# A transformer block on one core: x in four loads, LN1's norms on the vector engine, fp32 dummy matmuls, an earlier gate, and one earlier LN2 chunk

## The chip, the cores and the metric

The kernel runs on one core of a Trainium2 chip. Times are device microseconds (us) of one execution. The granted clock is the share of PE's full clock that the chip let it have, read from the profile: 1.0 is full. "Faster" or "slower" needs 2%; effects here are read as ratios to the kernel before, run on the same chip in the same rounds.

Engines: PE is the tensor engine (PEld its weight loads), DVE the vector engine, ACT the scalar engine, POOL the GpSimd engine, SP the engine that issues most transfers. "Modulating" is the multiplication by 1 + scale after a layer norm (in LN2 the shift is added too). A "fall" is a stretch in which the granted clock drops to a half. The "chain" is the work that ended last, followed back in the profile from the last instruction to what released each step.

## The reference

A DiT block with x of 2 x 256 x 1152 in bf16 (512 tokens, in four tiles of 128), two heads and a hidden size of 4608:

```python
mod = (_silu(c) @ w_mod).reshape(B, 6, 1, D)
shift_a, scale_a, gate_a, shift_m, scale_m, gate_m = [mod[:, i] for i in range(6)]
h = _layernorm(x) * (1 + scale_a) + shift_a            # LN1
q, k, v = split(h @ wqkv)
a = softmax(q k^T * Dh**-0.5) v @ wo
x = x + gate_a * a
h2 = _layernorm(x) * (1 + scale_m) + shift_m           # LN2
return x + gate_m * (_gelu(h2 @ w_fc1) @ w_fc2)
```

(The attention and split lines are shortened.)

## The kernel before

In the traces of this case DVE and ACT take up their instructions in program order (under e11, ACT starts tile 1's root 1.24 us later, behind its passes over tile 2; in the changed kernel DVE does four norms, 1.43 us, before the modulate that PE waits for). All weights stream through five buffers of 2.65 MB. Dummy matmuls, whose results nobody reads, are there to keep PE busy until its first inputs land (in the profile they run from 1.20 to 6.69 us, and the first scale weights land at 9.05). The parts that matter here (short statements joined on one line and comments added, cuts marked):

```python
for t in range(TPB):                                   # tiles 0, 1
    nc.sync.dma_start(x_sb[:, t, :], x_v[:, 0, t, :])
nc.sync.dma_start(x_sb[:, TPB:2 * TPB, :], x_v[:, 1, :, :])   # tiles 2 and 3 together
...
def warm(n, dst):                                      # dummy matmuls on zeros
    for _ in range(n):
        nc.tensor.matmul(dst[:], zeros[:, 0:P], zeros[:], start=True, stop=True)
warm(4, pwarm)
... # transpose of c, silu
def norm1(t, c0, c1, eng):                             # (x - mean) * rstd
    eng.tensor_scalar(xns[t][:, c0:c1], x_sb[:, t, c0:c1], mv1[:, t, 0:1], rstd1[:, t:t + 1],
                      op0=ALU.subtract, op1=ALU.mult)
...
CUT = 2 * P
warm(13, pwarm)
for j in range(NPD): stats_piece(0, j)                 # DVE bn_stats of tile 0
sqrt1(0); stats_piece(1, 0); recip1(0)
norm1(0, 0, CUT, nc.vector); norm1(0, CUT, D, nc.gpsimd)
act_stats(ACT.Identity, dsum)                          # tile 2's sums, on ACT
stats_piece(1, 1); stats_piece(1, 2); sqrt1(1)
act_stats(ACT.Square, dsq)
stats_piece(3, 0); recip1(1)
norm1(1, 0, CUT, nc.vector); norm1(1, CUT, D, nc.gpsimd)
stats_piece(3, 1)
add = scale_group(0)                                   # PE: 18 two-column matmuls
pt_a = transpose_x([0, 1], BT[0]); add()               # PE transposes of chunks 0, 1
modulate(pt_a, 0, 0, 0, 0, "d"); modulate(pt_a, 1, 1, 0, 0, "a")
... # statistics and first norms of tiles 3 and 2
k_step(0, 0, N); k_step(1, 0, N)                       # K projection, chunk by chunk
```

A K step multiplies one 128-column chunk of the modulated input with six weight blocks. Later, gate_a is computed in the V stage (after eight of twelve V groups), goes through DRAM to be broadcast to all partitions, and multiplies the output projection's result, from which LN2's statistics come:

```python
for i, (pnl, t) in enumerate(v_order):
    ...
    v_group(pnl, t)
    if i == 7:
        gate_a = gate_natural(0, w_gate_a)
...
BETWEEN = {2: ((0, "d"), (1, "d"), (2, "a"), (3, "a")), 3: ((8, "d"),)}   # LN2 modulates
...
nc.vector.tensor_tensor(tmp[:], pacc[:], gate_a[:, b, c0:c1], op=ALU.mult)
```

Of the kernel before, what the change touches and what calls it, by code (L numbers as in the profile page):

```python
# [8 lines left out]
FP32 = mybir.dt.float32  # L9
BF16 = mybir.dt.bfloat16  # L10
ACT = mybir.ActivationFunctionType
# [8 lines left out]
def kernel(  # L20
# [11 lines left out]
    nc = tc.nc  # L32
    B, N, D = x.shape
# [3 lines left out]
    P = 128  # L37
    T = B * N
    NT = T // P
    TPB = N // P  # L40
# [19 lines left out]
    def acc_tile(shape, name, dt=FP32):  # L60
        return psum.tile(shape, dt, name=name, tag="acc", bufs=6)

    def aux_tile(shape, name, dt=FP32):
        return psum.tile(shape, dt, name=name, tag="aux", bufs=2)


    x_v = x.rearrange("b (p l) d -> p b l d", l=TPB)
# [4 lines left out]
    wmod_v = w_mod.rearrange("(k p) n -> p k n", p=P)  # L72
# [3 lines left out]
    S_SHIFT_A, S_SCALE_A, S_GATE_A, S_SHIFT_M, S_SCALE_M, S_GATE_M = range(6)  # L76

    def wide_tile(name):
        return wide.tile([P, KD, D], BF16, name=name, tag="wide")


    x_sb = act.tile([P, NT, D], BF16, name="x_sb", tag="x_sb")
    c_sb = act.tile([B * KD, P], BF16, name="c_sb")
    nc.scalar.dma_start(c_sb[:], c_v)
    for t in range(TPB):
        nc.sync.dma_start(x_sb[:, t, :], x_v[:, 0, t, :])
    nc.sync.dma_start(x_sb[:, TPB:2 * TPB, :], x_v[:, 1, :, :])

    zeros = const.tile([P, T], BF16, name="zeros")
    nc.vector.memset(zeros[:], 0.0)  # L90
# [9 lines left out]
    KM1 = 6  # L100
# [17 lines left out]
    def load_rows(name, view, col0):  # L118
        w = wide_tile(name)
        for r in range(0, KD, 3):  # L120
            load = nc.sync.dma_start(w[:, r:r + 3, :], view[:, r:r + 3, col0:col0 + D])
            first_load.setdefault(name, load.ins)
        return w
# [5 lines left out]
    for (j0, j1), rows in zip(SHG, QROWS):  # L129
        nc.sync.dma_start(  # L130
            w_shift_a[:, :, j0 * P:j1 * P],
            wmod_v[:, :, S_SHIFT_A * D + j0 * P:S_SHIFT_A * D + j1 * P],
        )
        for r0, r1 in rows:
            nc.sync.dma_start(w_q[:, r0:r1, :], wqkv_v[:, r0:r1, 0:D])
    w_v = load_rows("w_v", wqkv_v, 2 * D)
    w_gate_a = load_rows("w_gate_a", wmod_v, S_GATE_A * D)
    w_o = load_rows("w_o", wo_v, 0)
    w_f1 = [None] * 4

# [15 lines left out]
    pwarm = acc_tile([P, T], "pwarm")  # L156


    def warm(n, dst):
        for _ in range(n):  # L160
            nc.tensor.matmul(dst[:], zeros[:, 0:P], zeros[:], start=True, stop=True)

    warm(4, pwarm)
    nc.tensor.transpose(pc[:], c_sb[:], ident[0:B * KD, 0:B * KD])
    nc.scalar.activation(
        sT[:, :, 0:B].rearrange("p k b -> p b k"), pc[:].rearrange("p (b k) -> p b k", b=B), ACT.Silu,
# [9 lines left out]
    def stats_piece(t, j):  # L176
        nc.vector.bn_stats(stats1[t][:, j, :], x_sb[:, t, j * PW:(j + 1) * PW])
        if j == NPD - 1:
            nc.vector.bn_aggr(mv1[:, t, :], stats1[t][:].rearrange("p a b -> p (a b)"))
# [4 lines left out]
    dsq = small.tile([P, 1], FP32, name="dsq", tag="dsq", bufs=1)  # L184
# [3 lines left out]
    def act_stats(f, dst):  # L188
        nc.scalar.activation(
            xns[T_ACT][:], x_sb[:, T_ACT, :], f, bias=pivot, scale=-1.0, accum_out=dst[:],  # L190
        )

    def act_stats_finish():
        nc.vector.scalar_tensor_tensor(
            dm2[:], dsum[:], -1.0 / (D * D), dsum[:], op0=ALU.mult, op1=ALU.mult
        )
        nc.vector.scalar_tensor_tensor(
            mv1[:, T_ACT, 1:2], dsq[:], 1.0 / D, dm2[:], op0=ALU.mult, op1=ALU.add
        )
        nc.vector.scalar_tensor_tensor(  # L200
            mv1[:, T_ACT, 0:1], dsum[:], -1.0 / D, pivot, op0=ALU.mult, op1=ALU.add
        )

    def sqrt1(t):
        nc.scalar.activation(rstd1[:, t:t + 1], mv1[:, t, 1:2], ACT.Sqrt, bias=eps_t[:], scale=1.0)

    def recip1(t):
        nc.vector.reciprocal(rstd1[:, t:t + 1], rstd1[:, t:t + 1])

    def norm1(t, c0, c1, eng):  # L210
        eng.tensor_scalar(
            xns[t][:, c0:c1], x_sb[:, t, c0:c1], mv1[:, t, 0:1], rstd1[:, t:t + 1],
            op0=ALU.subtract, op1=ALU.mult,
        )
# [22 lines left out]
    def modulate(pt, i, k, b, j0, eng):  # L237
        dst, src, sc = hT0[:, k, b * N:(b + 1) * N], pt[:, i, j0:j0 + N], scale_a[:, k, b:b + 1]
        if eng == "d":
            nc.vector.tensor_scalar_mul(dst, src, sc)  # L240
        else:
            nc.scalar.mul(dst, src, sc)
# [38 lines left out]
                start=(k == 0), stop=(k == KD - 1),  # L281
            )

    CUT = 2 * P
    BT = [range(b * TPB, (b + 1) * TPB) for b in range(B)]

    def both(pt, k):
# [6 lines left out]
    sqrt1(0)  # L294
    stats_piece(1, 0)
    recip1(0)
    norm1(0, 0, CUT, nc.vector)
    norm1(0, CUT, D, nc.gpsimd)
    act_stats(ACT.Identity, dsum)
    stats_piece(1, 1)  # L300
    stats_piece(1, 2)
    sqrt1(1)
    act_stats(ACT.Square, dsq)
    stats_piece(3, 0)
    recip1(1)
    norm1(1, 0, CUT, nc.vector)
    norm1(1, CUT, D, nc.gpsimd)
    stats_piece(3, 1)
    add = scale_group(0)
    pt_a = transpose_x([0, 1], BT[0])  # L310
    add()
    modulate(pt_a, 0, 0, 0, 0, "d")
    modulate(pt_a, 1, 1, 0, 0, "a")
    stats_piece(3, 2)
    sqrt1(3)
    act_stats_finish()
    sqrt1(2)
    recip1(3)
    norm1(3, 0, CUT, nc.vector)
    recip1(2)  # L320
    norm1(2, 0, CUT, nc.vector)
    k_step(0, 0, N)
    k_step(1, 0, N)
    pt_c = transpose_x([0, 1], BT[1])
# [5 lines left out]
    add()  # L330
    modulate(pt_b, 0, 2, 0, 0, "d")
    modulate(pt_b, 1, 3, 0, 0, "a")
    norm1(3, CUT, D, nc.vector)
    norm1(2, CUT, D, nc.vector)
    k_step(1, N, T)
    pt_d = transpose_x([2, 3], BT[1])
    modulate(pt_d, 0, 2, 1, 0, "d")
# [111 lines left out]
    def gate_natural(g, wg):  # L449
        pn = aux_tile([P, CTW], "pg")  # L450
        for k in range(KD):
            for i in range(4):
                nc.tensor.matmul(
                    pn[32 * i:32 * i + B, :], sT[:, k, 0:B], wg[:, k, i * CTW:(i + 1) * CTW],
                    start=(k == 0), stop=(k == KD - 1), tile_position=(0, 32 * i),
                )
        nat = work.tile([P, CTW], BF16, name="nat", tag="nat", bufs=1)
        for i in range(4):
            rows = slice(32 * i, 32 * i + B)
            if i % 2 == 0:  # L460
                nc.vector.tensor_copy(nat[rows, :], pn[rows, :])  # L461
            else:
                nc.scalar.copy(nat[rows, :], pn[rows, :])
            nc.gpsimd.dma_start(gates_dram[g, :, i * CTW:(i + 1) * CTW], nat[rows, :])  # L464
        return broadcast_gate(g)
# [4 lines left out]
    def q_mm(m, k):  # L470
        if k == 0:
            pq[m] = acc_tile([P, T], "pq")
        nc.tensor.matmul(  # L473
            pq[m][:], w_q[:, k, m * P:(m + 1) * P], hT[:, k, :],
            start=(k == 0), stop=(k == KD - 1), skip_group_check=True,
        )
        if k == KD - 1:
            evac(qT[:, m, :], pq[m][:], attn_scale)
# [7 lines left out]
    for m in range(KM1, KD):  # L486
        for k in range(KD):
            q_mm(m, k)

    def half(h):  # L490
        return slice(h * HP, (h + 1) * HP)
# [66 lines left out]
    for i, (pnl, t) in enumerate(v_order):  # L558
        if i < len(softmaxes):
            transposed = softmaxes[i]()  # L560
        v_group(pnl, t)
        if i == 7:
            gate_a = gate_natural(0, w_gate_a)

    w_shift_m = load_rows("w_shift_m", wmod_v, S_SHIFT_M * D)
    tc.add_manual_dep(first_load["w_shift_m"], transposed.ins.name, WAIT_FOR, reason="transposes first")
# [40 lines left out]
    def ln2_modulate(b, k, eng="d"):  # L607
        h = hT[:, k, b * N:(b + 1) * N]
        if eng == "a":
            return nc.scalar.activation(  # L610
                h, h, ACT.Identity, bias=shift_m[:, k, b:b + 1], scale=scale_m[:, k, b:b + 1],
            )
        return nc.vector.tensor_scalar(  # L613
            h, h, scale_m[:, k, b:b + 1], shift_m[:, k, b:b + 1], op0=ALU.mult, op1=ALU.add,
        )
# [34 lines left out]
        )  # L650


    BETWEEN = {2: ((0, "d"), (1, "d"), (2, "a"), (3, "a")), 3: ((8, "d"),)}

    def ln2_stats(t, i):
        nc.vector.bn_stats(stats2[t][:, i, :], x1[:, t, i * PW:(i + 1) * PW])  # L656
        if i == NPD - 1:
            nc.vector.bn_aggr(mv2[:, t, :], stats2[t][:].rearrange("p a b -> p (a b)"))
            ln2_normalize(t, t % 2 == 1, BETWEEN.get(t, ()))

    order = [(t, i) for t in range(NT) for i in range(NPD)]
    for o, (t, i) in enumerate(order):
        last = o == len(order) - 1
        if last:
            ln2_modulate(0, 4)
        wo_group(t, i, i < NPD - 1)
        if o == 2:
            vec_section(sT, w_shift_m, shift_m)
        if o == 5:
            vec_section(sT, w_scale_m, scale_m)  # L670
            nc.vector.tensor_scalar_add(scale_m[:, :, 0:B], scale_m[:, :, 0:B], 1.0)
        if o:
            ln2_stats(*order[o - 1])
        if last:
            ln2_modulate(0, 5, "a")
            ln2_modulate(0, 7, "a")
            ln2_modulate(0, 6)
    ln2_stats(*order[-1])
# [68 lines left out]
    for gi, (n, t, c0, cw) in enumerate(groups):  # L747
# [3 lines left out]
        for kk in range(KF):  # L751
# [4 lines left out]
                start=(kk == 0), stop=(kk == KF - 1),  # L756
# [11 lines left out]
    for ins in list(nc.cur_bb.bb.instructions)[first_traced:]:  # L768
        eng = ins.engine
# [38 lines left out]
```

## Time and profile before

249.81 us median of four runs (248.34 to 249.99). PE is busy for 237.6 of the 247.5 us span (96%). Of the rest, 3.6 us follow the last matmul; the waits that the profile names are listed here whole (engine, line, what it waited for: us in total, times, longest us):

```profile
PE pm L224 <- DMA w_scale_a<-in_w_mod_dram: 2.4, 1, 2.4
PE pwarm L161 <- DVE eps_t L94: 1.2, 1, 1.2
PE pacc L697 <- DVE hT L613: 0.6, 1, 0.6
PE pacc L697 <- ACT hT L610: 0.6, 1, 0.6
PE pk L250 <- DVE big L240: 0.5, 1, 0.5
PE pt L234 <- DVE xn L211: 0.5, 1, 0.5
```

The first line is PE waiting for the first scale weights after the dummies have run out. Lines 3 and 4 are waits of fc1 (L697) for LN2's modulates, lines 5 and 6 waits of the K stage.

The second loss doesn't show as idle time. In the view of windows of the kernel before, each line is one microsecond; after the length come the busy times of PE, PEld, DVE, ACT and POOL with their instructions, then the granted clock of PE, the share of the DMA engines and GB/s:

```profile
10.00:11.00 1.00, 0.58 (x6) 0.52 (x6) 0.95 (x3) 0.47 (x1) 1.00 (x1) 1.00 1.12 323
11.00:12.00 1.00, 1.00 (x8) 0.76 (x6) 0.84 (x7) 0.58 (x2) 1.00 (x1) 0.58 1.13 330
12.00:13.00 1.00, 0.54 (x4) 0.08 (x2) 0.83 (x3) 0.00 (x0) 0.79 (x1) 0.50 1.19 304
...
17.00:18.00 1.00, 0.99 (x8) 0.75 (x8) 0.29 (x2) 0.00 (x0) 0.00 (x0) 0.51 1.23 334
18.00:19.00 1.00, 1.00 (x11) 0.90 (x10) 0.13 (x1) 0.47 (x1) 0.00 (x0) 1.00 1.15 252
```

From within the second window on, PE works at half its clock, and is "busy" all the same. A K step of six 128x256 matmuls takes 1.44 us there.

Around LN2, from the timeline (up to 110 us; start, us, engine, line, operation, and in brackets the idle time before it and what ended it):

```profile
86.34 1.02 DVE L647 TENSOR_TENSOR tmp<-pacc,gate 128x384 f32<-128x384 f32 x2 [4.92 <-DMA gate<-gates_dram]
...
102.10 3.43 PE L697 MATMUL pacc<-hT,w_f 128*128 128x256 bf16 x30 [0.62 <-DVE hT L613]
...
106.10 4.09 PE L697 MATMUL pacc<-hT,w_f 128*128 128x256 bf16 x36 [0.57 <-ACT hT L610]
```

DVE can't start on the output projection's results until the gate arrives at 86.3 us, though the first result was there 3.7 us earlier (at 82.6); it is still behind when fc1 starts, and PE waits twice.

### The profile page before, as it was taken

To read this page: it belongs to the slowest core of one execution; us is meant where nothing else is said; L and a number is where in the kernel's file an instruction comes from. 1 tells how busy PE (TensorE), PEld (TensorE's weight loads), DVE (VectorE), ACT (ScalarE), POOL (GpSimd) and SP (SyncE) were. 2 spreads that over 40 slices of the span, in tenths; PEclk is the share of its full clock that TensorE was granted. 3 is DMA by queue.
4 is the path that set the end of the run, shared out by engine and by line. 5 is a ranking of instruction groups with operands and counts; after the bars stand their busy time and mean duration, and the time that the engine had idled before them with its cause. 6 is when DMAs were issued, how large, how long until landed. Compare 5 with 4: busy or idle time off the path is not lost.

```text
span 247.5 us, 3960 instructions
## 1 busy us (share of the span) xinstructions
PE 237.6 (96%) x1685; PEld 142.7 (58%) x1695; DVE 92.7 (37%) x199; ACT 61.1 (25%) x118; POOL 32.2 (13%) x39
## 2 busy tenths in 40 slices
PE   8599999999999999899999999999999999999994
PEld 2366444456657656678864444444566666666673
DVE  4842452316434189943000999970011000000001
ACT  5622431235134313455322333222000000000000
POOL 1900000000031043300000000001021222111111
PEclk9959999999999999999999999999999999999999
DMA  6999999992469999256999999199730000000000
GB/s 227 324 313 332 378 373 391 390 391 85 68 213 399 390 393 206 48 98 223 389 391 392 358 326 329 33 322 327 209 111 16 19 17 16 19 16 20 27 19 17
DMA packets 48637, 53.29 MB, mean 215 GB/s; under 512 B 9571, under 2 KB 36459, under 8 KB 48619
## 3 DMA queue, kind: packets, MB, share of 16 engines
q1 hardware_dynamic: 41168, 50.14, 60.3%
q10 hardware_dynamic: 6939, 1.71, 4.5%
q0 software_dynamic: 512, 1.19, 1.4%
q8 instruction: 13, 0.21, 0.4%
q14 instruction: 5, 0.04, 0.1%
HBM read 50.14 MB, written 1.19 MB: 207 GB/s over the span
## 4 chain that ended last, share of the span: by engine, by line
PE 79%; DMA 9%; DVE 5%; ACT 2%; issue 1%; POOL 1%; ACTq 1%; SPq 0%; DVEq 0%; POOLq 0%
PE pacc L753 28%; PE pacc L697 27%; PE pq L473 7%; PE pk L250 5%; PE pacc L550 5%; DMA w_scale_a<-in_w_mod_dram 3%; DMA gate<-gates_dram 3%; PE pk L279 2%; DMA gates_dram<-nat 2%; PE ps_s L508 2%; DMA hT<-xn 1%; DVE tmp L647 1%; PE pt L234 1%; DVE stats L656 1%; ACT xn L632 1%
## 5 line engine op out<-in xcount | busy, mean ns | idle before, releaser
L697 PE MATMUL pacc<-hT,w_f 128*128 128x256 bf16 (+1 forms) x427 | 70.4, 325 | 1.5 <-DVE hT L613 0.6
L753 PE MATMUL pacc<-w_f,gT 128*128 128x384 bf16 (+2 forms) x468 | 70.5, 314 | 0.0
L753 PEld LDWEIGHTS <-gT 128*128 128x128 bf16 x468 | 44.4, 98 | 26.3
L697 PEld LDWEIGHTS <-w_f 128*128 128x128 bf16 x432 | 42.2, 98 | 29.1 <-issue 1.7
L759 DVE TENSOR_TENSOR tmp<-pacc,gate 128x384 f32<-128x384 f32 (+2 forms) x13 | 6.9, 527 | 65.6 <-PE pacc L753 54.9
L729 ACT ACTIVATE gT<-pacc 128x512 bf16<-128x512 f32 x24 | 14.3, 597 | 32.6 <-PE pacc L697 32.6
L424 DVE SCALAR_TENSOR_TENSOR part<-w_gate_m,s,part 128x1152 f32<-128x1152 bf16 x16 | 21.4, 1413 | 0.0
L761 POOL TENSOR_TENSOR o_sb<-tmp,x 128x384 bf16<-128x384 f32 (+1 forms) x12 | 11.7, 973 | 51.4 <-DVE tmp L759 51.4
L642 PE MATMUL pacc<-w_o,big 128*128 128x384 bf16 x108 | 18.1, 326 | 0.0
L550 PE MATMUL pacc<-w_v,hT 128*128 128x384 bf16 x108 | 17.9, 326 | 0.0
L473 PE MATMUL pq<-hT,w_q 128*128 128x512 bf16 x79 | 17.7, 379 | 0.1
L250 PE MATMUL pk<-big,w_k 128*128 128x256 bf16 (+1 forms) x70 | 15.0, 364 | 0.6 <-DVE big L240 0.5
L550 PEld LDWEIGHTS <-hT 128*128 128x128 bf16 x108 | 10.4, 98 | 7.2 <-issue 0.5
L642 PEld LDWEIGHTS <-big 128*128 128x128 bf16 x108 | 10.3, 98 | 7.3 <-issue 0.7
L473 PEld LDWEIGHTS <-w_q 128*128 128x128 bf16 x81 | 7.9, 98 | 9.4
L250 PEld LDWEIGHTS <-w_k 128*128 128x128 bf16 x72 | 7.7, 111 | 4.7 <-issue 0.6
L464 POOL DMA_DIRECT2D gates_dram<-nat x4 | 2.3, 574 | 59.2 <-DVE nat L461 59.2
L446 POOL DMA_DIRECT2D gates_dram<-nat_v x2 | 1.1, 534 | 68.0 <-DVE nat_v L444 68.0
L422 DVE TENSOR_SCALAR part<-w_gate_m,s 128x1152 f32<-128x1152 bf16 x2 | 1.6, 817 | 22.2 <-DMA w_gate_m<-in_w_mod_dram 22.2
L648 POOL TENSOR_TENSOR x<-tmp,x_sb 128x384 f32<-128x384 f32 x8 | 7.3, 912 | 16.0 <-DVE tmp L647 16.0
L718 ACT ACTIVATE gT<-pacc 128x512 bf16<-128x512 f32 x12 | 6.5, 598 | 9.0 <-PE pacc L697 9.0
L647 DVE TENSOR_TENSOR tmp<-pacc,gate 128x384 f32<-128x384 f32 x12 | 6.4, 544 | 4.9 <-DMA gate<-gates_dram 4.9
(92 smaller groups left out, 167.8 us busy)
## 6 DMA issues: line engine op xcount, KB each, us to landing
w_f<-in_w_fc_dram SPq DMA_DIRECT2D x12, 864.0 KB, 15.0
w_f<-in_w_fc_dram SPq DMA_DIRECT2D x3, 1728.0 KB, 7.8
w_f<-in_w_fc_dram SPq DMA_DIRECT2D x2, 2592.0 KB, 19.7
w_v<-in_wqkv_dram SPq DMA_DIRECT2D x3, 864.0 KB, 12.6
w_gate_a<-in_w_mod_dram SPq DMA_DIRECT2D x3, 864.0 KB, 15.0
w_o<-in_wo_dram SPq DMA_DIRECT2D x3, 864.0 KB, 14.1
w_shift_m<-in_w_mod_dram SPq DMA_DIRECT2D x3, 864.0 KB, 6.6
w_scale_m<-in_w_mod_dram SPq DMA_DIRECT2D x3, 864.0 KB, 11.3
```

Source lines behind the costliest of these rows:

```text
L250: nc.tensor.matmul(pk[m][:, c0:c1], w_k[:, k, m * P:(m + 1) * P], hT0[:, k, c0:c1], start=(k == 0 and c0 == 0), stop=(k == KD - 1), skip_g ...
L424: nc.vector.scalar_tensor_tensor(part[:, b, :], wg[:, k, :], s32[:, k, b:b + 1], part[:, b, :], op0=ALU.mult, op1=ALU.add,)
L473: nc.tensor.matmul(pq[m][:], w_q[:, k, m * P:(m + 1) * P], hT[:, k, :], start=(k == 0), stop=(k == KD - 1), skip_group_check=True,)
L550: nc.tensor.matmul(pacc[:], hT[:, k, t * P:(t + 1) * P], w_v[:, k, pnl * PW:(pnl + 1) * PW], start=(k == 0), stop=(k == KD - 1),)
L642: nc.tensor.matmul(pacc[:], aT[:, k, t * P:(t + 1) * P], w_o[:, k, c0:c1], start=(k == 0), stop=(k == KD - 1),)
L647: nc.vector.tensor_tensor(tmp[:], pacc[:], gate_a[:, b, c0:c1], op=ALU.mult)
L648: (nc.gpsimd if pool_add else nc.vector).tensor_tensor(x1[:, t, c0:c1], tmp[:], x_sb[:, t, c0:c1], op=ALU.add)
L697: nc.tensor.matmul(dst, w_f1[m // KD][:, k, ml * P:(ml + 1) * P], hT[:, k, c0:c1], start=start, stop=(k == KD - 1), **kw,)
L729: nc.scalar.activation(gT[:, m, :], pacc[:], ACT.Gelu_apprx_tanh)
L753: nc.tensor.matmul(pacc[:], gT[:, kk, t * P:(t + 1) * P], w_f2[j][:, r, c0 - n * PW:c0 - n * PW + cw], start=(kk == 0), stop=(kk == KF - 1),)
L759: nc.vector.tensor_tensor(tmp[:], pacc[:], gate_m[:, b, c0:c0 + cw], op=ALU.mult)
L761: (nc.vector if last else nc.gpsimd).tensor_tensor(o_sb[:], tmp[:], x1[:, t, c0:c0 + cw], op=ALU.add)
```

## The change

Five edits. x comes in four loads, so that tile 2 is there before tile 3. LN1's norms are all on DVE: 512 columns of each tile first, the other 640 columns of all four tiles later. The dummies use fp32 zeros, to take longer and fill the wait for the scale weights. gate_a's weights load before w_v and the gate is computed in Q's last panels. Chunk 5 of LN2 is modulated earlier on ACT.

```diff
-    for t in range(TPB):
-        nc.sync.dma_start(x_sb[:, t, :], x_v[:, 0, t, :])
-    nc.sync.dma_start(x_sb[:, TPB:2 * TPB, :], x_v[:, 1, :, :])
+    for t in range(NT):
+        nc.sync.dma_start(x_sb[:, t, :], x_v[:, t // TPB, t % TPB, :])
...
+    w_gate_a = load_rows("w_gate_a", wmod_v, S_GATE_A * D)
     w_v = load_rows("w_v", wqkv_v, 2 * D)
-    w_gate_a = load_rows("w_gate_a", wmod_v, S_GATE_A * D)
...
+    zeros32 = zeros[:].bitcast(FP32)
-            nc.tensor.matmul(dst[:], zeros[:, 0:P], zeros[:], start=True, stop=True)
-    warm(4, pwarm)
+            nc.tensor.matmul(dst[:, 0:T // 2], zeros32[:, 0:P], zeros32, start=True, stop=True)
+    warm(2, pwarm)
...
-    CUT = 2 * P
+    CUT = 4 * P
...
-    norm1(0, 0, CUT, nc.vector)
-    norm1(0, CUT, D, nc.gpsimd)
+    norm1(0, 0, CUT)
     act_stats(ACT.Identity, dsum)
+    act_stats(ACT.Square, dsq)
... (statistics, roots and norms of tiles 1 to 3 reordered; first modulate from "d" to "a")
     modulate(pt_b, 1, 3, 0, 0, "a")
-    norm1(3, CUT, D, nc.vector)
-    norm1(2, CUT, D, nc.vector)
+    for t in range(NT):
+        norm1(t, CUT, D)
     k_step(1, N, T)
     pt_d = transpose_x([2, 3], BT[1])
     modulate(pt_d, 0, 2, 1, 0, "d")
...
             q_mm(m, k)
+        if m == KM1 + 1:
+            gate_a = gate_natural(0, w_gate_a)
...
-        if i == 7:
-            gate_a = gate_natural(0, w_gate_a)
...
-    BETWEEN = {2: ((0, "d"), (1, "d"), (2, "a"), (3, "a")), 3: ((8, "d"),)}
+    BETWEEN = {2: ((0, "d"), (1, "d"), (2, "a"), (3, "a"), (5, "a")), 3: ((8, "d"),)}
...
-            ln2_modulate(0, 5, "a")
```

More of the change, by code (lines that the diff above doesn't have):

```diff
@@ L208, in recip1, with norm1 @@
         nc.vector.reciprocal(rstd1[:, t:t + 1], rstd1[:, t:t + 1])
-    def norm1(t, c0, c1, eng):
-        eng.tensor_scalar(
+    def norm1(t, c0, c1):
+        nc.vector.tensor_scalar(
             xns[t][:, c0:c1], x_sb[:, t, c0:c1], mv1[:, t, 0:1], rstd1[:, t:t + 1],
@@ L302 @@
     sqrt1(1)
-    act_stats(ACT.Square, dsq)
     stats_piece(3, 0)
+    stats_piece(3, 1)
+    act_stats_finish()
     recip1(1)
-    norm1(1, 0, CUT, nc.vector)
-    norm1(1, CUT, D, nc.gpsimd)
-    stats_piece(3, 1)
+    norm1(1, 0, CUT)
+    sqrt1(2)
     add = scale_group(0)
@@ L311 @@
     add()
-    modulate(pt_a, 0, 0, 0, 0, "d")
+    modulate(pt_a, 0, 0, 0, 0, "a")
     modulate(pt_a, 1, 1, 0, 0, "a")
+    recip1(2)
     stats_piece(3, 2)
     sqrt1(3)
-    act_stats_finish()
-    sqrt1(2)
+    norm1(2, 0, CUT)
     recip1(3)
-    norm1(3, 0, CUT, nc.vector)
-    recip1(2)
-    norm1(2, 0, CUT, nc.vector)
+    norm1(3, 0, CUT)
     k_step(0, 0, N)
```

## The prediction

> **What bounds the kernel now.** The tensor engine (PE): the page gives it 237.6 of 247.5 us busy (96%), and 79% of the chain that ended last. Its idle time (timeline, PE's waits): 1.2 us at the start, 2.4 for the first scale weights (6.7 to 9.1 us), 0.47 for the first modulate, 0.46 for the norm of tiles 2/3, 0.62 and 0.57 before fc1 (101.5 to 106.1), 3.6 after the last matmul. "Busy" hides one more loss: the windows view shows a granted clock of 0.50 from 11.8 to 18.0 us; six 128x256 matmuls of a K step take 1.3 to 1.5 us there, six of the same shape in fc1 about 0.67. That costs about 6.2 x 0.5 = 3.1 us.
>
> **Why the clock drops.** The dummies end at 6.7; until 10.4 come only the wait, 18 two-column matmuls and four transposes. [...]
>
> **The change, costed.**
> 1. fp32 dummies. [...] The weights land at 9.05 today, so the gap closes and the clock should stay 1.0.
> 2. Four x loads: one more issue (0.47 us), but the DMA share is about 1.0 from 3 us on, so the scale weights land at 9.0 to 9.4. Tile 2's statistics start sooner.
> 3. Norms: two POOL norms of 3.4 us go. DVE does 512 columns of each tile first, and four 640-column pieces (about 0.4 us each) between two modulates: the second half of K step 2 will wait for DVE, 0.5 to 1 us. Tile 1's square root now follows both ACT passes on tile 2 (1.25 us each): first transposes 0.3 to 0.5 us later. So Q starts 2.1 us earlier, not 3.5.
> 4. A cap: shift_a's first load lands at 30.7 us (issue 17.6 + 13.1) and is used at 33.06, so at most 2.4 us can be gained before Q.
> 5. gate_a: the same 1.27 us of PE, moved. The gate lands at 86.2 today, could be used from 82.6, and DVE lags until fc1. Earlier by over 10 us, both waits before fc1 (0.62 + 0.57) should go; chunk 5 sooner helps the second. About 1.1 us. w_v in the later slot lands near 54, needed near 57: no wait.
>
> Sum: 2.1 + 1.1 = 3.2 us, from about 249.5.
>
> **Prediction:** 246.3 us, 8 in 10 between 244.9 and 248.3. Faster by over 2%: 0.09; within 2%: 0.89; slower by over 2%: 0.02.
>
> **What would show it.** Right: dummies busy until about 9.3; clock 1.0 from 9 to 18; 256-column K steps near 0.7 us; PE waiting for DVE once between 15 and 16.7; Q's first matmul near 33.6 (today 35.75); gate landed before 75; no PE wait over 0.2 us between wo and fc1. Wrong: dummies that end near 6.7 or well past 9.5; a 0.5 clock anywhere from 9 to 18; a PE wait for shift_a, w_q or w_v.
>
> **What would make it wrong.** The clock drops anyway in the thin stretch from 9.3 to 11 (then about 1.5 us in all); longer fp32 dummies delay the scale group; DVE in its new order holds PE longer; the four loads delay every weight load; w_v is late.

The sum came to 2.1 + 1.1 = 3.2 us, from about 249.5 to 246.3. What carried the 2.1 us, dummies that end near 9.3 us and a clock that then stays at 1.0, is no more than my estimate, not shown when it was made.

## The result

246.76 us median of four runs (246.02 to 247.12), against 249.81 before. The ratio is 0.9884, 95% interval 0.9845 to 0.9923: within 2%, but clear of 1. A second measurement of the same kernel later gave 0.9894.

PE's waits in the changed kernel, again the whole list:

```profile
PE pwarm L162 <- DVE eps_t L93: 1.2, 1, 1.2
PE pk L251 <- DVE big L241: 0.6, 1, 0.6
PE pk L251 <- ACT big L243: 0.6, 1, 0.6
```

The wait for the scale weights and both waits before fc1 are gone. The windows of the changed kernel show the full clock where the old one had half:

```profile
11.00:12.00 1.00, 0.88 (x23) 0.72 (x22) 0.33 (x3) 0.07 (x1) 0.00 (x0) 1.00 1.10 341
12.00:13.00 1.00, 0.55 (x6) 0.49 (x6) 0.87 (x4) 0.96 (x3) 0.00 (x0) 1.00 1.17 306
13.00:14.00 1.00, 1.00 (x14) 0.92 (x12) 0.57 (x2) 0.00 (x0) 0.00 (x0) 1.00 1.17 309
...
17.00:18.00 1.00, 0.41 (x5) 0.22 (x3) 0.70 (x3) 0.27 (x1) 0.00 (x0) 1.00 1.13 332
```

A K step of six 128x256 matmuls now takes 0.82 us. But the start of the chain (start, us, what) shows where that gain went:

```profile
3.39 7.81 PE pwarm L162 x26
11.20 0.43 PE pm L225 x18
...
14.59 0.81 PE pk L251 x6
...
16.02 1.43 DVE xn L212 x4
17.44 0.27 DVE big L241
...
35.25 5.18 PE pq L472 x24
```

The dummies hold PE until 11.20 us; the scale group (pm) had started at 9.10 before. Then the four 640-column norms (xn, 1.43 us) stand on the chain, as PE waits for the modulate behind them. Q starts at 35.25 us on the chain, where it was 35.91 before: 0.66 us gained before Q.

In LN2 the answers to the three lines of before are:

```profile
82.11 0.56 DVE L646 TENSOR_TENSOR tmp<-pacc,gate 128x384 f32<-128x384 f32 x1 [1.36 <-PE pacc L641]
...
100.65 9.55 PE L695 MATMUL pacc<-hT,w_f 128*128 128x256 bf16 x86
```

DVE now waits for PE, not for the gate, and fc1 runs without a wait. From the start of Q (35.25) to the start of fc2 (171.37 on the chain) the changed kernel takes 136.12 us, the old one 137.64 (35.91 to 173.55): 1.52 us gained. So this pair of profiles has 0.66 us from before Q and 1.52 from LN2. Whether that split is that of every run is what the experiments ask.

### The profile page after: what moved, and what is told of

Its sections match the earlier page's. It is cut to its first block, busy times and chain, and to the rows that moved or that the text cites. A ratio compares the mean times of both kernels' runs of the same rounds, so it can differ in the third digit from the quotient of the medians.

```text
span 245.3 us, 3997 instructions
## 1 busy us (share of the span) xinstructions
PE 239.3 (98%) x1708; PEld 147.0 (60%) x1708; DVE 92.9 (38%) x200; ACT 61.4 (25%) x119; POOL 25.4 (10%) x37
## 4 chain that ended last, share of the span: by engine, by line
PE 97%; DVE 1%; ACT 0%; issue 0%; DVEq 0%
PE pacc L695 29%; PE pacc L751 29%; PE pacc L641 7%; PE pq L472 7%; PE pacc L551 7%; PE pk L251 4%; PE pwarm L162 4%; PE pk L280 2%; PE pa L589 2%; PE ps_s L509 2%; PE pn L370 2%; PE pm L225 1%; PE pt L235 1%; DVE xn L212 1%; PE pg L452 0%; DVE big L241 0%
## 5 line engine op out<-in xcount | busy, mean ns | idle before, releaser
L251 PE MATMUL pk<-big,w_k 128*128 128x256 bf16 (+1 forms) x72 | 13.3, 326 | 1.2 <-DVE big L241 0.6
L162 PE MATMUL pwarm<-zeros 128*128 128x256 f32 x30 | 10.0, 502 | 1.2 <-DVE eps_t L93 1.2
L251 PEld LDWEIGHTS <-w_k 128*128 128x128 bf16 x72 | 6.7, 97 | 4.9 <-issue 1.5
L162 PEld LDWEIGHTS pwarm<-zeros 128*128 128x128 f32 x30 | 7.5, 257 | 2.6 <-DVE eps_t L93 1.2
```

Of the source, the lines that this page charges most:

```text
L162: nc.tensor.matmul(dst[:, 0:T // 2], zeros32[:, 0:P], zeros32, start=True, stop=True)
L251: nc.tensor.matmul(pk[m][:, c0:c1], w_k[:, k, m * P:(m + 1) * P], hT0[:, k, c0:c1], start=(k == 0 and c0 == 0), stop=(k == KD - 1), skip_g ...
```

## The experiments

Every kernel below gave correct results. e1 to e4 ran in one call beside 11 runs of the kernel before, e5 to e8 in a second, e9 to e12 in a third.

### The gate alone, on the kernel before

```diff
+    w_gate_a = load_rows("w_gate_a", wmod_v, S_GATE_A * D)
     w_v = load_rows("w_v", wqkv_v, 2 * D)
-    w_gate_a = load_rows("w_gate_a", wmod_v, S_GATE_A * D)
...
+        if m == KM1 + 1:
+            gate_a = gate_natural(0, w_gate_a)
...
-        if i == 7:
-            gate_a = gate_natural(0, w_gate_a)
```

> The kernel before, with one part of the change: gate_a is computed at Q's end and its weights load ahead of w_v. Theory (the change's gain comes mostly from LN2, where the vector engine no longer starts late): the two PE waits before fc1 (0.62 and 0.57 us) go or nearly go, the kernel is 1.0 to 1.5 us faster than before (ratio about 0.995), nothing changes before Q, and the clock still falls to 0.5 from about 12 to 18 us. Rival (the gain comes from the full clock in the K steps): under 0.4 us faster, ratio 0.998 or more. The second wait, for chunk 5 on the scalar engine, could stay, because chunk 5 is not moved here.

Ratio 0.9963 (0.9922 to 1.0005), median 247.42 us: about 0.9 us, just under what was expected, and the interval touches 1. The wait for DVE before fc1 went; the one for ACT, for chunk 5, stayed at 0.3 us:

```profile
PE pacc L697 <- ACT hT L610: 0.3, 1, 0.3
```

The clock fell in five of the six runs (mean clock 0.986 twice, 0.993 three times); the one run with a mean clock of 1.0 took 246.94 us. That the number of falls differs from run to run was new.

### The dummies alone, on the kernel before

```diff
-            nc.tensor.matmul(dst[:], zeros[:, 0:P], zeros[:], start=True, stop=True)
-    warm(4, pwarm)
+            nc.tensor.matmul(dst[:, 0:T // 2], zeros32[:, 0:P], zeros32, start=True, stop=True)
+    warm(2, pwarm)
```

> The kernel before, with only the fp32 dummies (2 and 13). Theory: the clock stays at 1.0 from 9 to 18 us, but the 13 dummies take 0.61 us each and hold PE until about 11.2, while the scale weights land at about 9.05; so the scale group starts 2.1 us later than before, and of the 3.1 us of clock little is left: Q's first matmul 0.4 to 1.2 us earlier than before, ratio 0.996 to 0.999. Rival: the clock is worth its 3.1 us all the same, ratio under 0.990. Second rival: dummies cost as much as they bring, ratio 1.000.

Ratio 0.9992 (0.9959 to 1.0025), median 248.72 us. The clock was 0.997 or more in all six runs, as it should be, and still nothing was gained: the second rival. In its profile the scale group starts at 10.63 us on the chain, 1.5 us later than before, and Q 0.39 us earlier:

```profile
10.63 0.43 PE pm L226 x18
...
35.52 5.18 PE pq L475 x24
```

Two effects cancel here. The mean of these six runs is 248.65 us; the six runs of the kernel before that had no fall either have 247.84 (the table under the old bf16 dummies below). So the fp32 dummies cost about 0.8 us, and the falls that they avoid had cost 1.1 us on average.

### The changed kernel with 10 dummies instead of 13

```diff
-    warm(13, pwarm)
+    warm(10, pwarm)
```

> The changed kernel with 10 fp32 dummies instead of 13. Theory (three dummies too many hold PE from about 9.4 to 11.2 us): the scale group starts near 9.5 us, when its weights land, the clock stays 1.0, everything up to Q is about 1.5 us earlier and the kernel 1.2 to 1.7 us faster than the changed kernel, ratio to before about 0.983. A smaller gain, 0.5 to 1 us, would mean that shift_a's weights (landing near 31 us) or another load now hold PE. Rival (the dummies' length doesn't matter, PE waits for the vector engine or for loads anyway): no more than 0.3 us.

Ratio 0.9869 (0.984 to 0.9898), median 245.63 us. Against the changed kernel's 0.9884 and 0.9894 that is 0.15 to 0.25%, some 0.4 to 0.6 us by the ratios, 1.1 us by the means (245.60 against 246.67, in other rounds). That is the direction of the theory, but not its size of 1.2 to 1.7, and as the intervals overlap, the gain itself is not clear of the noise. In its profile the scale group starts at 9.59 us and the clock stays full.

### The changed kernel with the old bf16 dummies

```diff
-    zeros32 = zeros[:].bitcast(FP32)
-            nc.tensor.matmul(dst[:, 0:T // 2], zeros32[:, 0:P], zeros32, start=True, stop=True)
-    warm(2, pwarm)
+            nc.tensor.matmul(dst[:], zeros[:, 0:P], zeros[:], start=True, stop=True)
+    warm(4, pwarm)
```

> The changed kernel with the old bf16 dummies (4 and 13), all else as changed. Theory: the dummies end at 6.7, PE waits about 2.8 us, the clock falls to 0.5 near 12 us and comes back near 18, so the 256-column K steps take 1.3 to 1.5 us again; the scale group starts near 9.5 instead of 11.2, so the net loss against the changed kernel is only 0.3 to 1.2 us, ratio to before about 0.991 to 0.994. Rival (the clock doesn't matter or doesn't fall): faster than the changed kernel by 1 us or more, as the scale group starts 1.7 us sooner.

Ratio 0.9877 (0.9839 to 0.9915), median 245.39 us. My theory fell here. The clock did not fall in the profiled run, although PE stood idle for 2.28 us before the scale group:

```profile
9.33 0.60 PE L223 MATMUL pm<-sT,w_scale_a 128*128 128x2 bf16 x18 [2.28 <-DMA w_scale_a<-in_w_mod_dram]
...
12.89 0.82 PE L249 MATMUL pk<-big,w_k 128*128 128x256 bf16 x6
```

Four of the six runs had a mean clock of 1.0 and took 244.99 to 245.43 us; two had 0.993 and took 246.52 and 247.38. So the same kernel has runs with a fall and runs without one, and the fp32 dummies of the change (0.9884 and 0.9894) are not faster here than what they replaced (0.9877).

That sent me back to the clocks of the runs of the kernel before. The three calls have 33 of them:

| mean clock of the run | runs | mean time, us |
|---|---|---|
| 0.997 or more | 6 | 247.84 |
| 0.991 to 0.993 | 14 | 248.73 |
| 0.985 or 0.986 | 13 | 249.76 |

The mean of all is 248.97 us, so the falls cost the kernel before 1.1 us per run on average (248.97 - 247.84). The profile on which I had predicted is of the slowest class. Even that class is only 1.9 us above the first (249.76 - 247.84).

### The changed kernel with 24 bf16 dummies

```diff
-            nc.tensor.matmul(dst[:, 0:T // 2], zeros32[:, 0:P], zeros32, start=True, stop=True)
+            nc.tensor.matmul(dst[:], zeros[:, 0:P], zeros[:], start=True, stop=True)
...
-    warm(13, pwarm)
+    warm(24, pwarm)       # and 4 instead of 2 at first
```

> The changed kernel with bf16 dummies, 24 after the transpose of c instead of 13, so that they end near 9.2 us, when the scale weights land. Theory now (the clock falls by chance, only where PE is left idle for some 2.5 us, and what holds it up is being busy, in any type): mean clock 0.997 or more in every run, scale group near 9.4, 245.0 to 245.6 us, ratio to before about 0.986, a narrow spread. Rival [...]: some runs with a mean clock of 0.993 or 0.986, and those runs 1 to 2 us slower, as with 13 bf16 dummies.

(The 2.5 us of idle time in the expectation are my reading of the waits of 2.41 us before, with a fall, and of 2.28 in e4's profile, without one. The rival was that the dummies' fp32 type holds the clock.) The clock was 1.0 in all five runs, as expected: with e9's six below, none of eleven runs with long bf16 dummies had a fall, against two of six in e4. So in these eleven runs fp32 was not needed to hold the clock. The time was a miss: ratio 0.9894 (0.9859 to 0.9929), median 246.18 us, no better than the changed kernel. Its profiled run took 245.46 us, the others 246.04 to 246.39.

### Old LN1, and old gate, each in the kernel with 10 dummies

The first has x's loads, the norms on POOL and DVE, and LN1's order of before; the second the gate and chunk 5 of before.

```diff
 # e6: on the changed kernel with warm(10, pwarm)
+    nc.sync.dma_start(x_sb[:, TPB:2 * TPB, :], x_v[:, 1, :, :])
+    CUT = 2 * P
+    norm1(0, CUT, D, nc.gpsimd)          ... and all of LN1 up to scale_group(2) as before
 # e7: on the changed kernel with warm(10, pwarm)
+        if i == 7:
+            gate_a = gate_natural(0, w_gate_a)    ... w_v loaded first, chunk 5 at its old place
```

> The changed kernel with 10 fp32 dummies, and x's three loads, the norms (half on the Pool engine) and the whole order of LN1 as before. Compared with the changed kernel with 10 dummies (245.6 us). Theory: the new LN1 order brings 1.0 to 1.5 us at full clock (246.6 to 247.1 here, ratio about 0.991), as PE waits twice for late norms of tiles 1 and 2/3 in the old order. Rival (the norms on the vector engine give back what they bring, since PE waits 0.6 us for them in K step 2): within 0.3 us of 245.6.

> The changed kernel with 10 fp32 dummies, with gate_a back in the V stage (its weights after w_v) and chunk 5 back at its old place. Compared with 245.6 us. Theory: LN2 loses 1.2 to 1.6 us (246.8 to 247.2 here, ratio about 0.992), PE waits for the vector and the scalar engine before fc1 again, and nothing changes before Q. Rival (the gate's place does not matter once LN1 is fast): within 0.4 us of 245.6.

Old LN1: ratio 0.9912 (0.9877 to 0.9948). Against 0.9869 that is 0.43%, 1.1 us (0.9 by the means without the one run in which the clock fell): LN1's new order, with x's four loads, is worth about that. PE's waits in that kernel show the old order's price, two waits for norms (1.3 us together):

```profile
PE pt L236 <- DVE xn L213: 1.3, 2, 0.7
PE pwarm L163 <- DVE eps_t L94: 1.2, 1, 1.2
PE pk L252 <- DVE big L242: 0.5, 1, 0.5
```

Old gate: ratio 0.9927 (0.9891 to 0.9962). Against 0.9869 that is 0.58%, 1.4 us (1.2 by the means without the one run with a fall), and both waits before fc1 are back:

```profile
99.57 3.44 PE L696 MATMUL pacc<-hT,w_f 128*128 128x256 bf16 x30 [0.64 <-DVE hT L612]
103.58 2.67 PE L696 MATMUL pacc<-hT,w_f 128*128 128x256 bf16 x23 [0.57 <-ACT hT L609]
```

Both came out as the theory said. Their intervals overlap; the waits are what makes the direction firm, not the sizes.

### The four norms after the modulates

```diff
     modulate(pt_b, 1, 3, 0, 0, "a")
-    for t in range(NT):
-        norm1(t, CUT, D)
...
     modulate(pt_d, 1, 3, 1, 0, "a")
+    for t in range(NT):
+        norm1(t, CUT, D)
```

> The changed kernel with 10 fp32 dummies, and the four 640-column norms placed after the modulates of chunks 2 and 3 of the second batch rather than before. Compared with 245.6 us. Theory (PE's 0.6 us of wait for the vector engine in K step 2 is real loss): the wait goes and the kernel is 0.4 to 0.7 us faster, 244.9 to 245.2, ratio about 0.985. Rival (shift_a's or w_q's loads hold PE by then, or the wait comes back at chunk 4's transposes, which need the norms): within 0.2 us of 245.6, with a PE wait for a load or for the norms.

Ratio 0.9844 (0.9809 to 0.9878), median 244.73 us: 0.6 us better than with 10 dummies alone, as expected, though the intervals overlap. This is, by its mean, the fastest version, ahead of both kernels. PE's wait for DVE in K step 2 is gone from its list:

```profile
PE pwarm L162 <- DVE eps_t L93: 1.2, 1, 1.2
PE pm L225 <- DMA w_scale_a<-in_w_mod_dram: 0.8, 1, 0.8
PE pk L251 <- ACT big L243: 0.6, 1, 0.6
```

Its profiled run was the slowest of the six, 246.38 us: there the clock fell from 11.86 to 15.27 us, although after its first instruction PE had never stood still for more than 0.85 us.

### Both: 26 bf16 dummies and late norms

```diff
-    warm(13, pwarm)
+    warm(26, pwarm)       # bf16, and 4 instead of 2 at first; the norms as in e8
```

> The changed kernel with 4 and 26 bf16 dummies, which should end near 9.6 us, and the four 640-column norms after the modulates. Theory: PE has neither an idle stretch before the scale group nor the wait for the norms; clock 0.997 or more in all runs, 244.5 to 245.2 us, 1.5 to 2 us faster than the changed kernel of the same call, without the one slow run in six that 10 fp32 dummies had. Rival: clock falls in some runs all the same (mean clock 0.993 or less).

Ratio 0.9854 (0.9821 to 0.9888), median 245.84 us, no falls (all clocks 0.997 or more), and 0.94 us faster than the changed kernel by the means (245.63 against 246.58). The expected 1.5 to 2 us was a miss. Two runs took 244.9 us, three 246.0 to 246.2. Two profiles of this kernel show where such a difference comes from: the first, from which the numbers of e9 below are, has a span of 243.2 us, the second, which is the one kept with the run, 244.3 us. Their chains (first, then second):

```profile
3.20 6.39 PE pwarm L160 x26
...
33.10 5.18 PE pq L470 x24
```

```profile
3.21 7.63 PE pwarm L160 x26
...
34.24 5.18 PE pq L470 x24
```

The same 26 dummies take 1.24 us longer in the second, and Q starts 1.14 us later.

### Chunk 5 alone, and x's loads alone, put back

```diff
 # e10, on the changed kernel with warm(10, pwarm)
-    BETWEEN = {2: ((0, "d"), (1, "d"), (2, "a"), (3, "a"), (5, "a")), 3: ((8, "d"),)}
+    BETWEEN = {2: ((0, "d"), (1, "d"), (2, "a"), (3, "a")), 3: ((8, "d"),)}
 # e11, on the same
-    for t in range(NT): ...
+    for t in range(TPB): ...
+    nc.sync.dma_start(x_sb[:, TPB:2 * TPB, :], x_v[:, 1, :, :])
```

> The changed kernel with 10 fp32 dummies and only chunk 5's modulate back at its old place. Compared with 10 dummies alone (245.6 us, ratio 0.987). Theory (the scalar engine reaches chunk 5 only after the third tile's normalisation and its transpose's issue): a PE wait of 0.3 to 0.5 us for the scalar engine comes back in fc1, the kernel is 0.2 to 0.5 us slower than 245.6. Rival (the early gate alone suffices): no wait, no difference.

> The changed kernel with 10 fp32 dummies and x in three loads as before. Compared with 10 dummies alone (245.6 us). Theory: tile 2 lands with tile 3 near 6.9 us instead of 5.7, so the scalar engine's two passes end 1.2 us later, tile 1's square root and norm wait behind them, and the first transposes start 0.6 to 1 us later (about 10.4 to 10.8); the kernel is 0.4 to 0.9 us slower. Rival (the fourth load only delays the scale weights): the scale weights land 0.3 to 0.5 us sooner and the kernel is 0 to 0.3 us faster.

Chunk 5: the wait came back as expected, 0.3 us for ACT. The time, ratio 0.9875 (0.9845 to 0.9905) against 0.9869, is too close to tell.

x's loads: ratio 0.9933 (0.99 to 0.9967), 1.6 us worse than 0.9869, more than expected. It is even worse than the whole old LN1 (0.9912), though here the two intervals overlap. PE waits 0.9 us for tile 1's norm. The reason is in ACT's lines, first of the kernel with three loads, then of the one with four (both with 10 dummies):

```profile
7.89 1.25 ACT L191 ACTIVATE xn<-x_sb 128x1152 bf16<-128x1152 bf16 x1 [2.19 <-DMA x_sb<-in_x_dram]
...
10.53 0.61 ACT L207 ACTIVATE rstd<-mv,eps_t 128x1 f32<-128x1 f32 x2
```

```profile
6.66 1.26 ACT L190 ACTIVATE xn<-x_sb 128x1152 bf16<-128x1152 bf16 x1 [0.93 <-DMA x_sb<-in_x_dram]
...
9.29 0.62 ACT L206 ACTIVATE rstd<-mv,eps_t 128x1 f32<-128x1 f32 x2
```

In the new order the square root of tile 1 stands on ACT behind both passes over tile 2. With three loads tile 2 lands late, and tile 1's root waits with it, 1.24 us longer. Some of the 1.6 us is the clock: two of the six runs had 0.99 and 0.993; the other four had a mean of 247.31 us.

### The changed kernel again

> The changed kernel itself, unaltered, for comparison on this chip and for the clocks of six runs. Theory: mean clock 0.997 or more in every run, since the dummies last until 11.2 us; about 246.7 us, ratio to before about 0.989 to 0.992, with a smaller spread than the kernel before, whose runs have mean clocks of 1.0, 0.992 and 0.986.

Ratio 0.9894 (0.9858 to 0.9929), median 246.37 us, and no fall of the clock. The chain of this second profile of the same program begins otherwise than that of the first:

```profile
3.39 6.54 PE pwarm L162 x26
9.93 0.43 PE pm L225 x18
...
33.97 5.18 PE pq L472 x24
```

The same 26 instructions took 6.54 us here and 7.81 there, and Q starts 1.28 us earlier. The trace's clock records tell why. The paces below show that PE starts at half clock in these traces, although the windows read a granted clock of 1.00 there (from 3 to 7 us in the changed kernel); the first clock record, which grants the full clock, comes later, and I call that moment the release: at 7.42 us in the first profile, at 4.83 in this one, and at 6.27 in the kernel with the dummies alone, where the 26 took 7.25 us. Two of the three give the pace: 0.44 us for one instruction at half clock, 0.224 at full clock (from 4.03/h + 3.78/f = 26 and 1.44/h + 5.10/f = 26, the times before and after the release). The third confirms it: 2.88/0.44 + 4.37/0.224 = 26.1. A dummy of two instructions so takes 0.45 us at full clock, and how long thirteen last depends on the moment of release. In e9's second profile the release came at 7.04 us.

## Why the prediction was right, and where its parts were not

The total was right: 246.3 us predicted, 246.76 measured; the gain was 3.2 us predicted, 2.6 and 2.9 measured by the two ratios. The terms were not all of their predicted size.

**The fp32 dummies.** "Dummies busy until about 9.3" was mis-sized: 11.20 in one profile, 9.93 in the other, and the prediction had named dummies that end "well past 9.5" as a sign of being wrong. Q's first matmul came at 35.1 and 33.8 us, not at 33.6. The cost of one was not what failed most: a dummy takes 0.45 us at full clock (its two instructions of 256 columns 0.448 together), against 0.114 us for a 128x256 bf16 matmul of fc1 (3.43 us for 30), a factor of 3.9, and with a release at 4.33 us the measured paces would have ended the dummies near 9.7 us (estimate from 0.44 and 0.224 us for one instruction). What failed most is the start: I took the release from half clock from the profile before (4.33 us), as if it were fixed. In the 14 kept profiles it comes between 4.33 and 7.81 us. The 3.1 us from there until 7.42, at half pace, add the other 1.5.

**The clock.** "That costs about 6.2 x 0.5 = 3.1 us" counts what PE lost, and a little low: the fall came at 11.16, not at 11.8 as I had read from the window with 0.58, so it is 6.82 x 0.5 = 3.4. It was wrong as the price that a run pays. The runs with a mean clock of 0.985 or 0.986, the class of that profile, are 1.9 us slower than those without a fall, and over 33 runs the mean price is 1.1 us. Two steps failed: taking lost clock for lost time, and reading one profile as the typical one. A part of the first is likely that a slower PE waits less: 0.5 us for LN1's norms (xn) in the profile before, 1.3 us in e2 and e6, which have the same order at full clock. Where the rest goes is open. Clock and dummies together were to give most of 2.1 us before Q; done alone they gave a ratio of 0.9992.

**Why the clock falls.** I held the thin stretch after the dummies responsible (6.69 to 10.42 us in the profile before), by a rule that no trace shows. What the traces show is when it falls. All four falls that were traced (before, e1, e8, e11) come 6.83 us after the release: 11.16 after 4.33, 12.55 after 5.73, 11.86 after 5.03, 12.32 after 5.49. They last 6.83 us in the first two and 3.41 in the others; in the ten other traces the full clock lasts 235.5 or 238.9 us after the release. One idle gap alone doesn't explain it: the clock fell with none over 0.85 us (e8) and stayed full with one of 2.28 (e4). So I counted what PE did in the last 3.41 us before that moment, from 3.41 to 6.83 us after the release (the stretch, as long as the shorter falls, is my choice). Of dense matmuls (dummies and K steps, not the two-column matmuls, not transposes) those with a fall had 0.74 us (before), 0.64 (e1), 1.15 (e8) and 0.07 (e11); three without had 1.14 (e4), 1.20 (e3) and about 1.5 (e7), the seven others 1.5 to 2.3. Of all that PE did there, two-column matmuls and transposes too, it was 1.1 to 2.0 us with a fall, 2.0 to 2.9 without. So the falls go with less work in that stretch, but e4 and e8 differ by 0.01 us of dense matmuls, the wrong way round. These are counts from fourteen traces, not an experiment that moved only this work: why the clock falls, and which work counts, is not shown.

**The norms.** "The second half of K step 2 will wait for DVE, 0.5 to 1 us" was right: 0.59 us, and e8 got 0.6 us back. "First transposes 0.3 to 0.5 us later" did not happen in the first profile: tile 1's norm was done by 9.4 us, and PE came for it at 11.5. With x in three loads it did happen, as e11 shows. That LN1's new order is worth about 1 us of its own (e6) I had not put into the sum; I had it give back part of the clock's gain.

**The cap.** "At most 2.4 us can be gained before Q" was wrong. I had taken shift_a's weights to land at 30.7 us whatever happens. In e9's first profile PE used them at 30.24 without a wait, and Q's first matmul started at 32.94, 2.8 us sooner than before. The landing is not a constant of the program.

**The gate and LN2.** The mechanism was right, the size low: 1.1 us predicted, 1.52 in the first pair of profiles and 1.4 by e7. The gate was requested at 59.7 us and took about 3.8 us to land, long before 75. Of the 1.4, chunk 5 takes away a wait of 0.3 us. w_v came in time: V ran without a wait, as predicted.

So the sum was right because errors cancelled, which is luck. Predicted was 2.1 before Q and 1.1 in LN2. By the ratios, 1.4 us are the gate with chunk 5, 1.1 us LN1 with x's four loads, 0.2 us or nothing the 13 fp32 dummies: 2.7 us, where the two measurements of the change give 2.6 and 2.9 (1 - 0.9894 and 1 - 0.9884 of 249 us). That these parts simply add up is not shown: two were taken out of the kernel with 10 dummies, one was put into the kernel before, and each ratio is uncertain by about 0.9 us.

The release also settles why e9 has runs of 246 us at full clock beside runs of 245: in its two profiles 1.24 us of longer dummies make 1.1 us of span. For e5 it is likely: its one profile, released at 4.49 us, is of its fastest run (245.46 us), but none of its four runs of 246 us was traced.

## What to carry to other kernels

Before predicting from a profile, look at the spread of all runs and their clocks: one profile showed 3.4 us of lost clock, of which runs of its kind lose 1.9 us and the average run 1.1. Dummy matmuls that must last until some transfer lands should be counted for the latest release of the clock as well as the earliest (7.81 and 4.33 us here), since those too many delayed what follows (in e2's profile the scale group started 1.5 us later), and those too few cost a fall in some runs only (two of six in e4, 1.7 us by the means). The release alone can move a run by up to 1.7 us (estimate: half of 7.81 - 4.33), more than half of what this change gains (2.9 us by its ratio), and between e9's two profiles it made 1.1 us of span, so changes of this size can't be judged without it. And an instruction moved behind others on an engine that takes them in program order, as ACT did here, inherits their wait (1.24 us in e11): the new LN1 order was good only together with the earlier load of tile 2.
